# Gate and value of ten pair-stages by seven quarter products, with x, y and the second layer's weights held in DRAM

## The chip, the cores and the metric

The kernel runs on one core of a Trainium2 chip. Five engines work side by side, each through its own queue in order: TensorE (PE in the rows) multiplies matrices into PSUM, VectorE (DVE) and ScalarE (ACT) do elementwise work and are the ones here that read PSUM, GpSimd (POOL) does a little elementwise work on SBUF, and SyncE (SP) issues the DMAs. They wait for each other by semaphores. The time is device microseconds (us) of one execution; the kernel before took 1267.62 us, the median of three runs (1266.94 to 1268.63).

## The reference

One layer of channel attention, and two gated layers one after the other, in float32. N is 6016 tokens, C is 256 channels, d_ff is 1536.

```python
qn = q / (norm(q, axis=tokens) + 1e-6); kn = k / (norm(k, axis=tokens) + 1e-6)
a = softmax(kn.T @ qn / tau, axis=-1)               # 256 x 256
x = v @ a                                           # 6016 x 256
xn = x / sqrt(mean(x * x, axis=-1) + 1e-6) * rms_g  # layer 1
g = xn @ w_gate; y = (silu(g) * (xn @ w_val)) @ w_out
g = y @ w_gate2; out = (sigmoid(g) * (y @ w_val2)) @ w_out2   # layer 2
```

## The kernel before

**Tiles.** The 47 tiles of 128 tokens are cut into twelve blocks: eleven of 512 tokens and one (block 5) of 384. d_ff is cut into twelve slices f of 128. Activations stand transposed, channels on partitions, in two halves c of 128. Every float32 operand of a product is split into a high part, rounded to the multiplier's format by a cast on ACT, and a low part, the rest, subtracted on DVE; a product is three matmuls, high by high, high by low, low by high (`mm3`, lines 86 to 89).

**An item** is one block at one slice of one layer: 288 in all. `emit_gv` makes gate (two products, c = 0 and 1) and value (two) in PSUM banks `g` and `v`, twelve matmuls. `emit_h` takes silu or sigmoid of the gate on ACT (`sg`, L331), multiplies on DVE (L334), casts the hidden value to `hh` on ACT (L337) and subtracts `hl` on DVE (L342). `emit_o`, two items later (`SKEW`), adds the slice's share to the block's output: two products, six matmuls into `y` or `at` (the same `mm3` lines). After slice 11 `emit_evac` copies the two banks out, for layer 1 into `ymid`, which holds all of y in SBUF, for layer 2 into a tile that SP stores. `g` and `v` have two PSUM banks each, `y` and `at` two each: all eight.

**The head** scores k by q while they stream in, makes the softmax matrix (`a_h`, `a_l`, L498 and L499), and then x of blocks 0 and 1. x of a block: `load_v`, split of v (L201, L207), 24 matmuls of 256 columns (L221 to L223), squares with a running sum on ACT (L244), mean on DVE (`ms`, L246), power on POOL (`rs`, L249), scaling (L255, L257), eight transposes (L274), split with rms_g (L282, L284). Blocks 2 to 11 do this between the items of the block before, by `hooks` on item numbers.

**Weights** come as 64-bit floats and are converted on the chip, one slice at a time: three passes on ACT (L119, L123, L136), four on DVE (L129, L139, L144, L147), then the split (L154 on ACT, L159 on DVE). `queue` cuts this into steps, and `pump` emits one to three steps an item. Layer 1's twelve conversions lie in the first 24 items, where blocks 0 and 1 take turns; layer 2's lie in the last two blocks of layer 1. The order of each engine is the order in which the code is written (`manual_schedule`).

## Time and profile before

| | us |
|---|---|
| Median of three runs | 1267.62 |
| The profiled execution, reported time | 1269.37 |
| Its span, first to last instruction | 1267.6 |
| PE busy | 1249.1 (99%) |
| DVE, ACT, POOL busy | 594.8 (47%), 517.1 (41%), 20.7 (2%) |

The reported time of the profiled execution is 1.77 us more than its span, and 1.75 us more than the median. A matmul's recorded time includes its way through the array, so records overlap; the distance from start to start is what a matmul costs in a row of them. The mean clock granted to PE is 0.997 of full.

### The profile page before, as it was taken

The numbers are of one execution on the slowest core, as the hardware profiler recorded it, in microseconds if no ns is written. First come the engines' busy times: TensorE is split into PE (matmuls) and PEld (weight loads), VectorE is DVE, ScalarE is ACT, GpSimd is POOL, SyncE is SP. The second block draws the span as 40 slices with busy tenths as digits, with TensorE's granted clock in tenths as the row PEclk, the third lists the DMA queues.
The fourth block names the chain that finished last, engine by engine and source line by source line (L and its number), as shares of the span: only waits on it lengthen the run. The fifth ranks groups of instructions, "written<-read, shape, count | busy, mean of one in ns | idle before, by whom it ended". The sixth has DMA issues, their size and how long they took to land.

```text
span 1267.6 us, 14204 instructions
## 1 busy us (share of the span) xinstructions
PE 1249.1 (99%) x5758; PEld 1049.7 (83%) x5758; DVE 594.8 (47%) x858; ACT 517.1 (41%) x907; POOL 20.7 (2%) x35
## 2 busy tenths in 40 slices
PE   8889999999999999999999999999999999999998
PEld 7767788888998888888888888888888888888888
DVE  6878643333434434334688534333433333333333
ACT  6766443333333333334567423333333323233332
POOL 0100000000000000000000000000000000000000
PEclk9999999999999999999999999999999999999999
DMA  9523000000000002000222000000000000000000
GB/s 335 213 92 117 18 13 1 18 1 17 17 1 18 17 1 92 1 1 1 67 88 70 1 1 17 17 18 1 17 17 1 17 17 1 17 18 1 17 17 13
DMA packets 15953, 44.42 MB, mean 35 GB/s; under 512 B 1808, under 2 KB 3344, under 8 KB 15888
## 3 DMA queue, kind: packets, MB, share of 16 engines
q1 hardware_dynamic: 15744, 43.39, 9.8%
q8 instruction: 45, 0.74, 0.3%
q14 instruction: 20, 0.16, 0.0%
q10 hardware_dynamic: 144, 0.13, 0.0%
HBM read 37.36 MB, written 6.16 MB: 34 GB/s over the span
## 4 chain that ended last, share of the span: by engine, by line
PE 91%; DVE 3%; ACT 3%; DMA 2%; issue 1%; SPq 0%; POOL 0%; DVEq 0%
PE g L89 10%; PE v L89 10%; PE v L87 10%; PE v L88 10%; PE g L87 10%; PE g L88 10%; PE y L89 9%; PE y L88 9%; PE y L87 9%; DMA in<-in_q_dram 2%; PE y L398 1%; PE at L88 1%; PE at L89 1%; PE at L87 1%; PE at L221 1%
## 5 line engine op out<-in xcount | busy, mean ns | idle before, releaser
L334 DVE TENSOR_TENSOR v<-v,sg 128x512 f32<-128x512 f32 (+1 forms) x288 | 198.0, 687 | 430.8 <-PE v L89 405.2
L337 ACT CAST hh<-v 128x512 fp32r<-128x512 f32 (+1 forms) x288 | 166.4, 578 | 405.7 <-DVE v L334 405.7
L331 ACT ACTIVATE sg<-g 128x512 f32<-128x512 f32 (+1 forms) x288 | 170.0, 590 | 282.5 <-PE g L89 282.4
L342 DVE TENSOR_TENSOR hl<-v,hh 128x512 fp32r<-128x512 f32 (+1 forms) x288 | 195.6, 679 | 149.2 <-ACT hh L337 148.5
L89 PE MATMUL y<-hh,wl 128*128 128x512 f32 (+1 forms) x504 | 193.6, 384 | 0.0
L88 PE MATMUL y<-hl,wh 128*128 128x512 f32 (+1 forms) x504 | 193.5, 384 | 0.0
L87 PE MATMUL y<-hh,wh 128*128 128x512 f32 (+1 forms) x504 | 193.4, 384 | 0.0
L87 PE MATMUL g<-xh,wh 128*128 128x512 f32 (+1 forms) x288 | 112.6, 391 | 5.7 <-ACT wh L154 5.0
L89 PE MATMUL g<-xh,wl 128*128 128x512 f32 (+1 forms) x288 | 111.9, 388 | 1.0 <-DVE wl L159 1.0
L88 PE MATMUL g<-xl,wh 128*128 128x512 f32 (+1 forms) x288 | 111.3, 386 | 0.3 <-DVE xl L284 0.3
L87 PE MATMUL v<-xh,wh 128*128 128x512 f32 (+1 forms) x288 | 111.1, 386 | 0.0
L89 PE MATMUL v<-xh,wl 128*128 128x512 f32 (+1 forms) x288 | 111.0, 385 | 0.0
L88 PE MATMUL v<-xl,wh 128*128 128x512 f32 (+1 forms) x288 | 111.0, 385 | 0.0
L88 PE MATMUL g<-yl,wh 128*128 128x512 f32 (+1 forms) x288 | 110.7, 384 | 0.0
L89 PE MATMUL g<-yh,wl 128*128 128x512 f32 (+1 forms) x288 | 110.7, 384 | 0.0
L87 PE MATMUL g<-yh,wh 128*128 128x512 f32 (+1 forms) x288 | 110.7, 384 | 0.0
L87 PE MATMUL v<-yh,wh 128*128 128x512 f32 (+1 forms) x288 | 110.7, 384 | 0.0
L88 PE MATMUL v<-yl,wh 128*128 128x512 f32 (+1 forms) x288 | 110.7, 384 | 0.0
L89 PE MATMUL v<-yh,wl 128*128 128x512 f32 (+1 forms) x288 | 110.7, 384 | 0.0
L89 PEld LDWEIGHTS y<-hh,wl 128*128 128x128 f32 x504 | 94.6, 188 | 17.8
L88 PEld LDWEIGHTS y<-hl,wh 128*128 128x128 f32 x504 | 94.6, 188 | 17.8
L87 PEld LDWEIGHTS y<-hh,wh 128*128 128x128 f32 x504 | 94.6, 188 | 17.7
(109 smaller groups left out, 1464.2 us busy)
## 6 DMA issues: line engine op xcount, KB each, us to landing
wraw<-in_w_dram SPq DMA_DIRECT2D x24, 768.0 KB, 4.3
vraw<-in_v_t_dram SPq DMA_DIRECT2D x11, 512.0 KB, 3.8
out_t_dram<-y SPq DMA_DIRECT2D x11, 512.0 KB, 2.7
in<-in_k_dram SPq DMA_DIRECT2D x13, 384.0 KB, 6.4
in<-in_q_dram SPq DMA_DIRECT2D x13, 384.0 KB, 6.7
in<-in_k_dram SPq DMA_DIRECT2D x4, 128.0 KB, 3.9
in<-in_k_dram SPq DMA_DIRECT2D x2, 256.0 KB, 6.3
in<-in_q_dram SPq DMA_DIRECT2D x2, 256.0 KB, 6.4
```

What stands on the lines that cost most here:

```text
L87: nc.tensor.matmul(ps, sh, mh, start=start, stop=False)
L88: nc.tensor.matmul(ps, sh, ml, start=False, stop=False)
L89: nc.tensor.matmul(ps, sl, mh, start=False, stop=stop)
L221: nc.tensor.matmul(ps, h[:, c, ts], a_h[:, c], start=c == 0, stop=False)
L331: nc.scalar.activation(out=sg[:, :w], in_=gp[:, :w], func=(AF.Silu, AF.Sigmoid)[l])
L334: nc.vector.tensor_mul(vp[:, :w], vp[:, :w], sg[:, :w])
L337: nc.scalar.copy(hh[:, :w], vp[:, :w])
L342: nc.vector.tensor_sub(hl[:, :w], vp[:, :w], f32(hh[:, :w]))
L398: nc.tensor.matmul(s_ps[c][:, :C], qk[i0][0][:, i, c * P : (c + 1) * P], qk[i0][1][:, i], start=(i0 + i == 0), stop=(i0 + i == NT - 1),)
```

## The change

Two neighbouring blocks make a pair of 1024 tokens (the pair with block 5: 896), cut into two halves e of 512 (448). With the weights of gate and value as a 2 by 2 matrix of 128 by 128 quarters (A11, A12 gate; A21, A22 value) and the pair's input as a 2 by 2 matrix of quarters (B11, B12, B21, B22: channel half by token half), gate and value of both halves were eight quarter products. They become seven, in Winograd's form of Strassen's scheme, with sums of weight quarters (S1 to S4, made once a slice) and of input quarters (T1 to T4, made once a pair). A **period** (function `period`) is one pair at one slice: seven products (21 matmuls) and the four output products of the period before (12 matmuls), 33 where two items had 36. Some of the sums over products are made by adding in PSUM (Z gets three products, B two), the others on DVE and ACT: a period has eight DVE operations and seven ACT operations on a half, where two items had four and four. In layer 1 the pairs 0 and 1 keep the old items (`plain_gv`, `plain_h`); pairs 2 to 5 of layer 1 and all six of layer 2 run in periods: 48 items and 120 periods.

- **x.** All twelve blocks make x at once, before the first item, in a loop over `blocks` (2 to 10, 0, 11, 1); the transposed, scaled block is written to DRAM (`xd`), and only blocks 0 and 1 stay. Later `q_load` and `pair_load` fetch it. All scaling is on DVE.
- **y** of layer 1 goes to DRAM (`yd`) by `evacuate`, four stores a pair, and is fetched by `pair_load` one pair ahead.
- **A pair's operands.** In the pair before: loads in period 0, three subtractions on POOL in period 2 (a fourth after T1's split), and seven splits, one a period, casts in periods 3 to 9 on ACT and subtractions in 4 to 10 on DVE.
- **Conversions.** All 24 run among the 48 items. Each gets four sums of 128 columns on POOL, two casts on ACT (384 and 128 columns) and two subtractions on POOL. The cast to high goes ahead of the next slice's first passes. Layer 2's converted slices go to DRAM (`w2d`) and are loaded back into the slots of layer 1's slices during that layer's last pair; layer 1's S3 goes to `s3d` and later takes the place of A21. Raw weights have two buffers where they had three.

```diff
-    order = [list(range(NB)), [b for b in range(NB) if b != short] + [short]]
...
+    A11, A12, A21, A22, OUT, S1, S2, S4 = 0, 1, 2, 3, 4, 6, 7, 8
+    S3 = A21
...
+        def sums():
+            t = w["t"]
+            w["s3"] = cv2.tile([P, 1, P], F32, tag="s3", name="s3")
+            nc.gpsimd.tensor_add(t[:, S1], t[:, A21], t[:, A22])
+            nc.gpsimd.tensor_sub(w["s3"][:, 0], t[:, A11], t[:, A21])
+            nc.gpsimd.tensor_sub(t[:, S2], t[:, S1], t[:, A11])
+            nc.gpsimd.tensor_sub(t[:, S4], t[:, A12], t[:, S2])
...
+            steps.append([high, size, units, shifted])
+            steps.append([low])
+            steps.append([s_high, whole, signed])
+            steps.append([s_low, rounded])
+            steps.append([guarded, ss[0], store])
+            if i + 2 < len(conversions):
+                steps[-1].append(partial(load_w, *conversions[i + 2]))
...
+    def pair_sums(l, p):
+        sums.clear()
+        pair_sum(l, p, T1, T3, B11)
+        pair_sum(l, p, T2, B22, T1)
+        pair_sum(l, p, T3, B22, T3)
...
+            Z = gv_bank("g")[:, :w]
+            product(Z, it, B11, A11, True)
+        if pv:
+            pl, pp, pf = pv["it"]
+            pw = hw[pp]
+            nc.vector.tensor_add(pv["g1"], pv["g1"], pv["B"])
+            hh0, hl0 = hidden("hh"), hidden("hl")
+            nc.scalar.copy(hh0[:, :pw], pv["v0"])
+            hid[pl, pp, 0, pf] = hh0, hl0
+        if it:
+            e1 = sp.tile([P, 512], F32, tag="e1", name="e1")[:, :w]
+            nc.scalar.copy(e1, Z)
+        if pv:
+            nc.vector.tensor_sub(hl0[:, :pw], pv["v0"], f32(hh0[:, :pw]))
+            nc.scalar.activation(out=pv["g1"], in_=pv["g1"], func=(AF.Silu, AF.Sigmoid)[pl])
+        if it:
+            A = gv_bank("v")[:, :w]
+            product(A, it, B21, A12, True)
+            nc.vector.tensor_add(A, A, e1)
+            B = s["B"] = gv_bank("g")[:, :w]
+            product(B, it, T1, S1, True)
+            sg0 = ip2.tile([P, 512], F32, tag="sg", name="sg")[:, :w]
+            nc.scalar.activation(out=sg0, in_=A, func=(AF.Silu, AF.Sigmoid)[l])
+        if pv:
+            nc.vector.tensor_mul(pv["v1"], pv["v1"], pv["g1"])
+        if it:
+            product(Z, it, T2, S2, False)
+        for fn in slot.get("DVE", ()):
+            fn()
+        if it:
+            s["g1"] = sp2.tile([P, 512], F32, tag="g1", name="g1")[:, :w]
+            nc.scalar.copy(s["g1"], Z)
+        if pv:
+            hh1, hl1 = hidden("hh"), hidden("hl")
+            nc.scalar.copy(hh1[:, :pw], pv["v1"])
+            nc.vector.tensor_sub(hl1[:, :pw], pv["v1"], f32(hh1[:, :pw]))
+            hid[pl, pp, 1, pf] = hh1, hl1
+        for fn in slot.get("ACT", ()):
+            fn()
+        if it:
+            D = s["v0"] = gv_bank("v")[:, :w]
+            product(D, it, T4, A22, True)
+        for o in outs[:1]:
+            o()
+        if it:
+            product(Z, it, T3, S3, False)
+            e3 = sp.tile([P, 512], F32, tag="e3", name="e3")[:, :w]
+            nc.scalar.copy(e3, Z)
+            s["v1"] = sp2.tile([P, 512], F32, tag="v1", name="v1")[:, :w]
+            nc.vector.tensor_add(s["v1"], B, e3)
+            nc.vector.tensor_sub(D, e3, D)
+        for o in outs[1:]:
+            o()
+        if it:
+            product(B, it, B22, S4, False)
+            nc.vector.tensor_mul(D, D, sg0)
...
+        for n, b in enumerate(blocks):
+            x_mm(b, row_banks(n))
+            if n > 1:
+                t_pe(blocks[n - 2])
+                if blocks[n - 2] > 1:
+                    t_out(blocks[n - 2], n % 2)
...
+            if n:
+                x_scale(blocks[n - 1])
+            if n + 2 < NB:
+                v_high(blocks[n + 2])
+                v_low(blocks[n + 2])
+            x_square(b)
+            if n + 3 < NB:
+                load_v(blocks[n + 3])
+            for fn in spare.pop(0) if spare else ():
+                fn()
...
+        stream = [(0, p, f) for p in range(PLAIN, NP) for f in range(NF)]
+        stream += [(1, p, f) for p in (0, 1, 3, 4, 5, 2) for f in range(NF)]
```

On PE, in the middle of layer 2, an item's last value product and an output product stood like this before (`yh`, `yl` are the block's input, high and low):

```order
L87 MATMUL v<-yh,wh 128x512
L88 MATMUL v<-yl,wh 128x512
L89 MATMUL v<-yh,wl 128x512
L87 MATMUL y<-hh,wh 128x512
L88 MATMUL y<-hl,wh 128x512
L89 MATMUL y<-hh,wl 128x512
```

and the middle of a period now (`xh`, `xl` an operand's parts; the products are S2 by T2 into Z, A22 by T4 into D, one output product, S3 by T3 into Z):

```order
L105 MATMUL g<-xh,wh 128x512
L106 MATMUL g<-xl,wh 128x512
L107 MATMUL g<-xh,wl 128x512
L105 MATMUL v<-xh,wh 128x512
L106 MATMUL v<-xl,wh 128x512
L107 MATMUL v<-xh,wl 128x512
L105 MATMUL y<-hh,wh 128x512
L106 MATMUL y<-hl,wh 128x512
L107 MATMUL y<-hh,wl 128x512
L105 MATMUL g<-xh,wh 128x512
L106 MATMUL g<-xl,wh 128x512
L107 MATMUL g<-xh,wl 128x512
```

The second visit to Z in one period stands nine matmuls after the first, with an ACT copy of the bank to be made between them; before, a bank was filled once and read once.

On DVE, before, x work of a block between the items of the block before it (`v` and `hl` are an item's two operations; POOL makes `rs` between `ms` and `xn`):

```order
L334 TENSOR_TENSOR v<-v,sg 128x512
L342 TENSOR_TENSOR hl<-v,hh 128x512
L246 TENSOR_SCALAR ms<-ssq 128x2 x2
L257 TENSOR_SCALAR xn<-at,rs 128x256 x2
L334 TENSOR_TENSOR v<-v,sg 128x512
L342 TENSOR_TENSOR hl<-v,hh 128x512
```

and now two rounds of the loop over blocks, ahead of the first item:

```order
L330 TENSOR_SCALAR xo<-y,g_sb 128x512 x2
L311 TENSOR_SCALAR xn<-at,rs 128x256 x4
L278 TENSOR_TENSOR vl<-vraw,vh 128x1024
L302 TENSOR_SCALAR ms<-ssq 128x4
L190 TENSOR_TENSOR wl<-wst,wh 128x768
L330 TENSOR_SCALAR xo<-y,g_sb 128x512
L311 TENSOR_SCALAR xn<-g,rs 128x256 x2
L311 TENSOR_SCALAR xn<-v,rs 128x256 x2
L278 TENSOR_TENSOR vl<-vraw,vh 128x1024
L302 TENSOR_SCALAR ms<-ssq 128x4
```

The x work has moved out of the stream of items into a stretch of its own, with a conversion's operation (`wl`) between rounds.

On DVE, one period of a pair now (where two items had `v`, `hl`, `v`, `hl`):

```order
L514 TENSOR_TENSOR hl<-v,hh 128x512
L519 TENSOR_TENSOR v<-v,e_6302 128x512
L525 TENSOR_TENSOR v_6274<-v_6274,g_6255 128x512
L363 TENSOR_TENSOR xl<-xl,xh 128x512
L536 TENSOR_TENSOR hl<-v_6274,hh 128x512
L550 TENSOR_TENSOR v_6340<-g,e_6338 128x512
L551 TENSOR_TENSOR v<-e_6338,v 128x512
L556 TENSOR_TENSOR v<-v,sg 128x512
L506 TENSOR_TENSOR g_6322<-g_6322,g 128x512
```

Eight operations of the period itself, and one split of the next pair (L363).

## Rows read from the trace of the kernel before

**Rows 1.** The page, busy time: engine, us (share of the span), instructions.
```profile
PE 1249.1 (99%) x5758; PEld 1049.7 (83%) x5758; DVE 594.8 (47%) x858; ACT 517.1 (41%) x907; POOL 20.7 (2%) x35
```

**Rows 2.** The page, the chain that ended last, share of the span by engine.
```profile
PE 91%; DVE 3%; ACT 3%; DMA 2%; issue 1%; SPq 0%; POOL 0%; DVEq 0%
```

**Rows 3.** Timeline, one item of layer 2: start, us, engine, line, operation [idle before].
```profile
899.90 0.39 PE L89 MATMUL v<-yh,wl 128*128 128x512 f32 x1
900.12 0.39 PE L87 MATMUL y<-hh,wh 128*128 128x512 f32 x1
...
900.38 0.70 DVE L334 TENSOR_TENSOR v<-v,sg 128x512 f32<-128x512 f32 x1 [2.04 <-PE v L89]
...
901.11 0.59 ACT L337 CAST hh<-v 128x512 fp32r<-128x512 f32 x1 [1.49 <-DVE v L334]
...
904.20 0.39 PE L87 MATMUL y<-hh,wh 128*128 128x512 f32 x1
```

**Rows 4.** Timeline, PE, one item of the 384-token block, from gate to gate.
```profile
1255.74 0.33 PE L87 MATMUL g<-yh,wh 128*128 128x384 f32 x1
...
1258.86 0.33 PE L87 MATMUL g<-yh,wh 128*128 128x384 f32 x1
```

**Rows 5.** Windows: us, busy of PE PEld DVE ACT POOL (instructions), clock, DMA, GB/s.
```profile
60.00:65.00 5.00, 4.04 (x17) 2.56 (x16) 3.75 (x8) 4.04 (x12) 1.21 (x2) 1.00 0.17 73
...
80.00:85.00 5.00, 5.00 (x19) 3.96 (x19) 3.37 (x5) 2.03 (x4) 0.00 (x0) 0.81 0.79 265
61.38:137.06 75.68, 68.26 (x287) 53.38 (x287) 61.54 (x87) 51.30 (x84) 1.36 (x2) 0.98 0.26 87
590.00:690.00 100.00, 100.00 (x449) 82.93 (x448) 74.53 (x104) 63.06 (x100) 1.39 (x2) 1.00 0.22 72
```

**Rows 6.** Timeline, from the softmax matrix to the first gate matmul, and one idle.
```profile
53.70 0.28 PE L221 MATMUL x<-a_h,vh 128*128 128x256 f32 x1
...
54.06 0.28 PE L221 MATMUL at<-a_h,vh 128*128 128x256 f32 x1
...
55.32 0.48 DVE L499 SCALAR_TENSOR_TENSOR a_l<-sc,rsum,a_h 128x256 fp32r<-128x256 f32 x1
...
61.38 0.50 PE L87 MATMUL g<-xh,wh 128*128 128x512 f32 x1 [0.67 <-ACT xh L282]
...
77.66 0.50 PE L87 MATMUL g<-xh,wh 128*128 128x512 f32 x1 [3.73 <-ACT wh L154]
```

**Rows 7.** The chain in order of time: a block's eight transposes.
```profile
168.81 0.87 PE at L274 x8
```

**Rows 8.** Groups by line and shape: count, busy us, mean ns, idle before.
```profile
L159 DVE TENSOR_TENSOR wl<-wst,wh 128x768 fp32r<-128x768 f32 x24 | 23.0, 958 | 21.8 <-ACT wh L154 21.6
...
L244 ACT ACTIVATE xn<-at 128x256 f32<-128x256 f32 x43 | 16.1, 382 | 19.3 <-PE at L223 19.3
...
L207 DVE TENSOR_TENSOR vl<-vraw,vh 128x1024 fp32r<-128x1024 f32 x11 | 13.5, 1224 | 6.4 <-ACT vh L201 6.4
...
L201 ACT CAST vh<-vraw 128x1024 fp32r<-128x1024 f32 x11 | 11.5, 1048 | 0.0
...
L257 DVE TENSOR_SCALAR xn<-at,rs 128x256 f32<-128x256 f32 x22 | 10.5, 481 | 4.3 <-POOL rs L249 4.3
```

**Rows 9.** Timeline, POOL beside DVE, two pairs of powers.
```profile
57.30 0.96 DVE L144 CUSTOM_DVE_ANT_0 wbits<-wbits,wunits 128x1536 uint16<-128x1536 uint16 x1
57.42 2.06 POOL L249 TENSOR_TENSOR rs<-ms,nhalf 128x2 f32<-128x2 f32 x2 [12.20 <-DVE ms L246]
...
63.80 1.36 POOL L249 TENSOR_TENSOR rs<-ms,nhalf 128x2 f32<-128x2 f32 x2 [4.31 <-DVE ms L246]
```

**Rows 10.** Groups by line and shape: POOL's widest operation.
```profile
L379 POOL MEMSET acc<- 128x1536 f32 x1 | 1.4, 1382 | 0.0
```

**Rows 11.** The page, DMA issues: count, KB each, median us to landing.
```profile
wraw<-in_w_dram SPq DMA_DIRECT2D x24, 768.0 KB, 4.3
vraw<-in_v_t_dram SPq DMA_DIRECT2D x11, 512.0 KB, 3.8
```

**Rows 12.** Timeline, the last matmul.
```profile
1263.88 0.34 PE L89 MATMUL y<-hh,wl 128*128 128x384 f32 x1
```

More of the change, by code (lines that the diff above doesn't have):

```diff
@@ new lines, with queue, nothing @@
+    conversions = [(l, f) for l in range(2) for f in range(NF)]
+    def queue(first, late):
+        def nothing():
+            pass
+        high, low, s_high, s_low, store = nothing, nothing, *late
+        for i, (l, f) in enumerate(conversions):
+            if i < first:
+                continue
+            (size, units, whole), (shifted, signed, rounded, guarded), hl, ss = conversion(l, f)
+            steps.append([high, size, units, shifted])
[5 more added lines that the diff above has]
+                steps[-1].append(partial(load_w, *conversions[i + 2]))
+            (high, low), (_, s_high, s_low, store) = hl, ss
+        steps.extend(([high], [low, s_high, s_low, store]))
@@ L246, in x_square @@
+    def x_square(b):
+        xn[b] = lent("xn").rearrange("p c t -> p (c t)").rearrange("p (i c) -> p i c", c=C)
+        ssq, ms, rs = xst[b] = [small.tile([P, TB], F32, tag=t, name=t) for t in ("ssq", "ms", "rs")]
+        for i in range(sizes[b]):
+            nc.scalar.activation(
+                out=xn[b][:, i], in_=xps[b][i // 2][:, i % 2], func=AF.Square, accum_out=ssq[:, i : i + 1]
+            )
+        cs = slice(0, sizes[b])
         nc.vector.tensor_scalar(
@@ new lines, in evacuate, with product, period @@
+        nc.sync.dma_start(out=dst, in_=t[:, :w])
+    slots = deque()
+    def product(ps, it, i, a, start):
+        l, p, f = it
+        h, lo = ops[l, p][i]
+        w = hw[p]
+        mm3(ps[:, :w], wh[l, f][:, a], wl[l, f][:, a], h[:, :w], lo[:, :w], start, True, not start)
+    def period(it, pv, outs, last=False):
+        s = {}
+        slot = slots.popleft() if slots else {}
+        outs = [partial(out_mm, *o, c) for o in outs for c in range(KC)]
+        if it:
+            l, p, f = it
+            w = hw[p]
+            s["it"] = it
+            Z = gv_bank("g")[:, :w]
[51 more added lines that the diff above has]
+            o()
+        if it:
+            product(B, it, B22, S4, False)
+            nc.vector.tensor_mul(D, D, sg0)
+        for fn in slot.get("end", ()):
+            fn()
+        return s
@@ L627 @@
+        for e in range(2):
+            for c in range(KC):
+                evacuate(*stream[-1][:2], e, c, c)
 def kernel(**inputs):
```

603 lines of the change are left out of this document (325 added, 278 removed).

## Prediction, made before the changed kernel was run

> **What bounds the kernel now.** I read the busy times first, then the chain of waits, then a timeline of one item, then windows. PE is busy for 1249.1 of 1267.6 us, DVE for 47% and ACT for 41% [rows 1], and PE holds 91% of the chain that ended last [rows 2]. So the end is set by how many matmuls there are and by the distance between them. That distance comes from one item: the same output matmul starts at 900.12 and at 904.20 [rows 3], so eighteen matmuls of 512 columns take 4.08 us, 0.2267 each. An item of 384 columns takes 1258.86 - 1255.74 = 3.12 us, 0.1733 each [rows 4]; half way, 448 columns are an estimated 0.200. In layer 2 PE never waits: DVE stands idle 2.04 us for PE's value in every item [rows 3]. What PE loses it loses at the start: from the first gate matmul at 61.38 to 137.06 it is busy for 68.26 of 75.68 us at a clock of 0.98 [rows 5], which is 7.4 us idle and 1.5 us of slow clock, because items wait for converted weights.
>
> **Term 1, the periods.** 96 periods are of 512 columns, 24 of 448. At PE's distance they take 96 x 33 x 0.2267 + 24 x 33 x 0.200 = 718.2 + 158.4 = 876.6 us. The same work in items took 96 x 8.16 + 24 x (4.08 + 3.12) = 956.2 us. The gain is 79.6 us, if PE does not wait inside a period.
>
> **Whether it waits.** I lay out one period by hand, t = 0 at its first matmul. A product is three matmuls, 0.68. From the timeline: a reader starts 0.25 after a product's slot ends (the last value matmul starts at 899.90, the next at 900.12, DVE at 900.38); a DVE operation takes 0.70 and an ACT operation 0.59; a handover costs 0.03 (DVE ends 901.08, ACT starts 901.11) [rows 3]. Independent operations of one engine overlap by 0.1. All forms in a period (PSUM with SBUF into either, a cast, an activation) stand in the trace at these durations.
> PE's slots: Z 0 to 0.68, A to 1.36, B to 2.04, Z again to 2.72, D to 3.40, output to 4.08, Z a third time to 4.76, three outputs to 6.80, B again to 7.48.
> - The copy e1 of Z runs 0.93 to 1.52; Z is written again at 2.04. Slack 0.52.
> - B of the period before ends at 0; g1 + B runs 0.25 to 0.95; B's bank is written at 1.36. Slack 0.41.
> - A + e1 starts at 1.61, ends 2.31; sg0 on ACT to 2.93; the copy g1 waits for Z (2.72 + 0.25), ends 3.56; Z is written at 4.08. Slack 0.52.
> - The copy e3 starts at 5.01, ends 5.60; v1 = B + e3 ends 6.33; B is written at 6.80. Slack 0.47.
> - hl0 ends 1.55 (needed at 3.40); hl1, after v1 x g1 (2.91) and hh1 (4.06), ends 4.78 (needed at 5.4).
> DVE's and ACT's own loop (v1, D, D x sg0, g1 + B, hl0, A + e1; sg0, g1, hh1, a split's cast, e3) is 3.9 + 2.7 + 0.1 = 6.7 us of 7.48. With an evacuation or a split in a period it still closes. So I take no wait in term 1. The other bound is that each slack is overrun by 0.1 to 0.35 us a period, 12 to 42 us in all; I take zero since every duration is a row of this trace. What hides the rest: the next pair's loads land (3.8 us for 512 KB [rows 11]) two periods before POOL wants them; the second layer's weights, two loads of 576 KB a period, are wanted eleven periods, 82 us, after they are asked for, against 4.3 us for 768 KB [rows 11]. SP issues in order and waits there for PE of the period just past; stores and loads behind it are late by a period at most, and none is wanted so soon.
>
> **Term 2, x ahead of everything.** `x_mm` now takes both channel halves tile by tile, so it starts in earnest when the second `a_l` is made, 55.32 + 0.48 = 55.8 [rows 6]; I take 55.3, since the first three matmuls go ahead. A block costs PE 24 x 0.12 (three matmuls from 53.70 to 54.06 [rows 6]) + 0.87 for transposes [rows 7] = 3.75 us. It costs DVE one or two `xo` of 0.70 [rows 3], four scalings of 0.39 in a row (0.48 each less the overlap), the split 1.14 (1.22 less it) [rows 8] and the mean, together 3.5 to 4.1; ACT, the cast 1.05 and four squares (0.38 each, with the accumulator's read in its gap) [rows 8], 2.6. A third loop goes over memory: `load_v` stands behind the store of `xo` on SP, lands 3.8 us later [rows 11], and the cast, squares, mean, power, scaling and transposes that follow on it are two rounds on: about 12.0 to 13.5 us for three rounds. The three limits are 3.75, 3.9 and 4.0 to 4.5; I take 4.3. The first two rounds fill until 55.3 + 3 x 2.88 + 0.87 + 0.2 = 65.0; nine rounds of 4.3 end at 103.7; four conversion operations of 0.95 on DVE [rows 8] between rounds add 3.8; block 0's split, block 1's scaling and block 11's transposes add 4.5. **First gate at 112.0**, where it was 61.38. Bounds: 103 (3.75 a round, conversions hidden) and 122 (loads at 6.5 us, 5.0 a round). In before ten blocks of this lay between items and cost PE 37 us there; so the move itself costs 13 us.
>
> **Term 3, the 48 items.** 48 x 4.08 = 195.8, and block 1's transposes 0.9. Conversions: the first gate needs slice f at item 1.6 f, that is every 6.5 us; before, PE lost 8.9 us there [rows 5]. Now the cast comes ahead of two ACT passes, which gives its low part earlier, and two more casts (about 0.7 us by ACT's rows) come into ACT; x no longer disturbs. I take 11 (bounds 0 and 30, see the first rival). Layer 2's twelve conversions lie in 24 items of 4.08, 8.2 us each, with DVE at 4.0 + 2 x 1.3 = 6.6; a denser run of them before left PE at 100.00 of 100 [rows 5]; I take 2. The first pair's operands are loaded five items ahead: 1.
>
> **Term 4, the end.** The last matmul ended at 1264.22 [rows 12], 3.4 us before the span did; that stays. The last period's outputs must wait for silu or sigmoid of the second half: g1 + B, activation, product, cast, subtraction, by the durations above 4.7 us with 2.4 us of matmuls in it: 2.3 us more. Together 5.7.
>
> **Sum.** 112.0 + 195.8 + 0.9 + 11 + 2 + 1 + 876.6 + 5.7 = 1205.0 us of span. The profiled execution's time is 1.77 above its span and 1.75 above the median, so span and median are the same number here: **1205 us**, 62.6 us or 4.9% less.
>
> **The rivals.**
> *POOL and DVE hold each other.* Every conversion now has six POOL operations on 1,024 columns beside DVE operations with two inputs in SBUF. The trace shows one side: a pair of powers took 2.06 us when its first began beside a DVE operation of two SBUF inputs, 57.30 to 58.26, and 1.36 elsewhere [rows 9]; the first waited 0.7 us. The trace has no row in which DVE waited, and none of POOL's additions. Bounds for six of them: 0.9 us at the memset's 0.9 ns a column [rows 10], 5.9 us at 0.68 an operation [rows 9] plus two memsets' rate. DVE is nearly full only in the first ten conversions; half of the middle, 1.7 us each, gives 17 us: 1222. The Trainium skill, page "SBUF — State Buffer", section "Who interferes with whom", says that a VectorE instruction with two SBUF inputs and a GpSimd instruction that reads SBUF exclude each other, and that the one that comes second waits to the end of the first; by that rule DVE would wait as POOL did, and the trace agrees for POOL's side.
> *The slack in a period is eaten.* Some wait of 0.1 to 0.35 us in each of 120 periods, at e1, g1, e3 or B: 1217 to 1247. For it: four places with half a microsecond. Against it: the layout above.
> *x at half clock.* After 3.73 us idle the clock fell (0.81 in 80 to 85) [rows 5, 6]. At 1.2 GHz a round is 7.5 us of PE, 9 x 3.2 = 29 us more: 1234. Against it: PE with idle pieces kept 1.00 from 60 to 65 [rows 5], and no idle in the loop is over 2 us.
> *Slower than before.* Seven ACT and eight DVE operations a period hang in one loop of eleven; PE pays for nothing while the loop is under 7.48 us. At 7.48 + 62.6/120 = 8.0 us the gain is gone. That needs 0.12 us more on each of the eleven than the rows show, as when PSUM is read twice as often beside PE's writes: at 8.1, 1279. Nothing in the trace shows such a stretch.
> *It does not do what it says:* the matmuls fall, but PE is bound elsewhere and the time stays within 0.2%. I find no such bound; it needs 0.5 us in each period exactly.
>
> **How the numbers follow.** My forecast, 1192 to 1218, has 0.62; POOL 0.14; slack 0.09; half clock 0.05; slower 0.07; the same 0.03. A difference under 0.2% cannot be told from none here. Faster by over 0.2%: 0.62 + 0.14 + 0.09 + 0.05 = 0.90. The range goes from 1190 (x at its lower bound, conversions at 6) to 1240, which takes in POOL, half clock and most of the slack case.
>
> **What would show it.** Right: matmul distances of 0.227 through a whole period, 7.48 us from one Z to the next; first gate near 112; PE idle in the x stretch about 15%. Wrong: PE waiting for `e1`, `g1`, `e3` or `v1` in the waits (term 1); rounds above 5 us, or PE waiting there for a v load (term 2); DVE operations at twice their length beside POOL (term 3). If periods take over 8 us, all of it is wrong.

## The result and the profile after

The changed kernel took 1215.45 us (median of four runs, 1215.33 to 1217.14) where the kernel before took 1268.12 beside it: a ratio of 0.9585, 95% interval 0.9566 to 0.9603. The gain is 52.7 us of the 62.6 that were forecast. The profiled execution, the longest of the four, reports 1217.14 us, with a span of 1215.3.

On the page, the busy times and the chain that ended last (they answer to [rows 1, 2]):

```profile
PE 1183.3 (97%) x5398; PEld 989.9 (81%) x5398; DVE 936.6 (77%) x1397; ACT 733.0 (60%) x1348; POOL 178.2 (15%) x207
...
PE 71%; DVE 1%; ACT 1%; DMA 0%; issue 0%; ACTq 0%; DVEq 0%
```

TensorE has 360 matmuls less, 65.8 us less of busy time, and still holds the chain (which could be followed back through 73% of the span). DVE, ACT and POOL have taken over the additions: 342, 216 and 158 us more.

One period of 512 columns in the middle of layer 2, from the timeline (start, duration, engine, line, operation, output and inputs; idle time before it in brackets). It answers to the item of [rows 3]:

```profile
735.79 0.39 PE L105 MATMUL g<-xh,wh 128*128 128x512 f32 x1
735.99 0.69 DVE L506 TENSOR_TENSOR g<-g,g 128x512 f32<-128x512 f32 x1
...
736.73 0.59 ACT L512 COPY e<-g 128x512 f32<-128x512 f32 x1
...
737.15 0.39 PE L105 MATMUL g<-xh,wh 128*128 128x512 f32 x1
...
737.83 0.39 PE L105 MATMUL g<-xh,wh 128*128 128x512 f32 x1
...
738.77 0.59 ACT L532 COPY g<-g 128x512 f32<-128x512 f32 x1
...
739.87 0.39 PE L105 MATMUL g<-xh,wh 128*128 128x512 f32 x1
...
740.81 0.59 ACT L548 COPY e<-g 128x512 f32<-128x512 f32 x1 [0.42 <-PE g L107]
...
741.43 0.69 DVE L550 TENSOR_TENSOR v<-g,e 128x512 f32<-128x512 f32 x1 [0.83 <-ACT e L548]
...
742.59 0.39 PE L105 MATMUL g<-xh,wh 128*128 128x512 f32 x1
...
743.27 0.39 PE L105 MATMUL g<-xh,wh 128*128 128x512 f32 x1
```

From the first Z at 735.79 to the next at 743.27 it is 7.48 us, 33 times 0.2267, and no matmul in it waits. The four places of the layout by hand can be read off (e1, g1 and e3 are ACT's copies of Z, v1 is the second half's value). The copy e1 ends at 737.32 and Z is written again at 737.83: 0.51 to spare (0.52 forecast). g1 + B ends at 736.68 and B is written at 737.15: 0.47 (0.41). The copy g1 ends at 739.36, Z is written at 739.87: 0.51 (0.52). v1 ends at 742.12, B is written at 742.59: 0.47 (0.47).

The stretch of the 48 items, from the first gate matmul (110.71) to the first Z (323.87), in windows (engine busy times and instruction counts, granted clock, DMA share, GB/s), and TensorE's waits in it (the wait for `hl` is for the bank `v`, which is free when `hl` has been read from it):

```profile
110.71:323.87 213.16, 202.81 (x863) 162.36 (x862) 173.46 (x225) 142.53 (x246) 109.77 (x141) 0.98 0.50 175
110.71:130.00 19.29, 16.32 (x65) 12.71 (x64) 14.67 (x21) 12.16 (x21) 8.62 (x11) 0.86 0.26 84
130.00:240.00 110.00, 102.62 (x430) 80.25 (x429) 96.90 (x119) 78.19 (x133) 63.28 (x82) 0.98 0.48 167
240.00:323.87 83.87, 83.87 (x372) 69.40 (x371) 61.89 (x86) 52.17 (x93) 37.88 (x48) 1.00 0.59 206
```

```profile
PE g L105 <- ACT wh L182: 5.2, 3, 2.1
PE v L105 <- DVE hl L451: 2.6, 4, 1.8
PE g L107 <- DVE wl L190: 2.5, 4, 0.9
```

All that is lost is lost before 240: TensorE is idle for 10.4 us there, and the granted clock is 0.86 and 0.98. How the idle time and the clock hang together is in one place of the timeline:

```profile
124.33 0.50 PE L105 MATMUL g<-qh,wh 128*128 128x512 f32 x1 [2.07 <-ACT wh L182]
...
125.97 0.61 PE L107 MATMUL g<-qh,wl 128*128 128x512 f32 x1 [0.90 <-DVE wl L190]
126.38 0.63 PE L105 MATMUL g<-qh,wh 128*128 128x512 f32 x1
126.80 0.63 PE L106 MATMUL g<-ql,wh 128*128 128x512 f32 x1
```

TensorE waits 2.07 us for the third slice's cast and 0.90 for its low part, and then its matmuls come 0.42 apart instead of 0.23, the lower of its two levels (1.2 GHz), until 129.4: after 3.0 us of waiting, eight matmuls that cost some 1.6 us more than in a period. Part of a wait there is paid a second time. In the kernel before the same stage lost 7.4 us idle at a clock of 0.98 [rows 5].

**The account** of the profiled span, with the forecast's terms cut at the same places (the last two items' twelve output matmuls lie in the first period, so the forecast's first Z is at 320.0, and the last period's outputs come after the last product):

| | forecast | measured | difference |
|---|---|---|---|
| First gate matmul | 112.0 | 110.71 | -1.3 |
| From there to the first Z | 208.0 | 213.16 | +5.2 |
| First Z to the end of the last product | 876.6 | 882.05 | +5.4 |
| From there to the end of the span | 8.4 | 9.4 | +1.0 |
| Span | 1205.0 | 1215.3 | +10.3 |

How much of this is chance can be read from the other profiled runs below. In the six with the same head and x stage (this one, e3_no_t4, e4_short, e7_e3x3, e8_whole_first, e11_late_high) the first gate matmul comes between 110.0 and 113.0. In the five with the same items (this one, e3_no_t4, e4_short, e5_loads, e7_e3x3) the stretch to the first Z is 212.3 to 213.9.

### The profile page after: what moved, and what is told of

The parts are those of the page before. It is cut to its first block, busy times and chain, and to the rows that moved or that the text cites. A ratio compares the mean times of both kernels' runs of the same rounds, so it can differ in the third digit from the quotient of the medians.

```text
span 1215.3 us, 15199 instructions
## 1 busy us (share of the span) xinstructions
PE 1183.3 (97%) x5398; PEld 989.9 (81%) x5398; DVE 936.6 (77%) x1397; ACT 733.0 (60%) x1348; POOL 178.2 (15%) x207
## 4 chain that ended last, share of the span: by engine, by line
PE 71%; DVE 1%; ACT 1%; DMA 0%; issue 0%; ACTq 0%; DVEq 0%
PE g L105 11%; PE g L106 11%; PE g L107 11%; PE at L106 4%; PE at L107 4%; PE at L105 4%; PE v L106 4%; PE v L107 4%; PE y L106 4%; PE v L105 4%; PE y L107 4%; PE y L105 4%; DMA out_t_dram<-yo 0%; DVE hl L536 0%; DVE v L556 0%
## 5 line engine op out<-in xcount | busy, mean ns | idle before, releaser
L508 ACT CAST hh<-v 128x512 fp32r<-128x512 f32 (+1 forms) x120 | 69.2, 577 | 237.9 <-DVE v L556 237.9
L536 DVE TENSOR_TENSOR hl<-v,hh 128x512 fp32r<-128x512 f32 (+1 forms) x120 | 89.1, 742 | 96.4 <-ACT hh L535 96.4
L105 PE MATMUL g<-qh,wh 128*128 128x512 f32 (+1 forms) x276 | 108.2, 392 | 5.2 <-ACT wh L182 5.2
L106 PE MATMUL at<-hl,wh 128*128 128x512 f32 (+1 forms) x288 | 111.9, 389 | 0.3 <-DVE hl L536 0.2
L105 PE MATMUL y<-hh,wh 128*128 128x512 f32 (+1 forms) x288 | 111.0, 386 | 0.7 <-ACT hh L508 0.7
L106 PE MATMUL y<-hl,wh 128*128 128x512 f32 (+1 forms) x288 | 111.0, 386 | 0.2 <-DVE hl L514 0.2
L105 PE MATMUL at<-hh,wh 128*128 128x512 f32 (+1 forms) x288 | 111.1, 386 | 0.0
L107 PE MATMUL at<-hh,wl 128*128 128x512 f32 (+1 forms) x288 | 111.0, 385 | 0.0
L107 PE MATMUL g<-qh,wl 128*128 128x512 f32 (+1 forms) x276 | 108.1, 392 | 2.5 <-DVE wl L190 2.5
L106 PE MATMUL g<-ql,wh 128*128 128x512 f32 (+1 forms) x276 | 107.3, 389 | 0.0
L105 PE MATMUL v<-qh,wh 128*128 128x512 f32 (+1 forms) x216 | 85.2, 394 | 2.6 <-DVE hl L451 2.6
L556 DVE TENSOR_TENSOR v<-v,sg 128x512 f32<-128x512 f32 (+1 forms) x120 | 82.3, 686 | 4.2
```

The source lines that it names most:

```text
L105: nc.tensor.matmul(ps, sh, mh, start=start, stop=False, skip_group_check=more)
L106: nc.tensor.matmul(ps, sh, ml, start=False, stop=False, skip_group_check=more)
L107: nc.tensor.matmul(ps, sl, mh, start=False, stop=stop, skip_group_check=more)
L508: nc.scalar.copy(hh0[:, :pw], pv["v0"])
L536: nc.vector.tensor_sub(hl1[:, :pw], pv["v1"], f32(hh1[:, :pw]))
L556: nc.vector.tensor_mul(D, D, sg0)
```

## Experiments

All times are medians, except where one run is named; ratios are to the kernel before, run on the same chip. The changed kernel's 1215.45 has 0.9566 to 0.9603, which is what each is to be held against.

### The items: GpSimd, then ACT

For its size, the term that was furthest off is that of the items. Two kernels take away what the sums of weights cost there, first GpSimd's part, then ACT's too.

In the first the six GpSimd operations go, and the casts read plain quarters (the low parts of the sums are then not stored and fetched either):

```diff
-            nc.gpsimd.tensor_add(t[:, S1], t[:, A21], t[:, A22])
...
-            nc.gpsimd.tensor_sub(t[:, S4], t[:, A12], t[:, S2])
...
-            nc.scalar.copy(h[:, S1:], w["t"][:, S1:])
+            nc.scalar.copy(h[:, S1:], w["t"][:, :3])
...
-            nc.gpsimd.tensor_sub(lo[:, S1:], w["t"][:, S1:], f32(h[:, S1:]))
...
-            nc.gpsimd.tensor_sub(w["3l"], w["s3"], f32(w["3h"]))
```

> Leaves out what GpSimd does in a weight conversion (four sums and two low parts, six operations of 128 to 384 columns); the casts on ACT stay and read the plain quarters instead, and the products take plain quarters, so the output is not the reference's. Theory 1 (VectorE waits for GpSimd): the shift, the sign operation and the low part fall from 726, 1115 and 1096 ns to the 552, 951 and 958 of the kernel before, 0.5 us a conversion; in the ten that feed the items this is on the path: the stretch from the first gate matmul to the first product falls from 213.3 to about 207, 1208 to 1211 us in all. Theory 2 (the loss is the length of the conversion chain itself, GpSimd only fills VectorE's gaps): within 1.5 us of 1215.4.

Measured: 1211.81 us, 0.9551 to 0.9577, which overlaps the changed kernel's interval, so the median alone doesn't show a gain. In the profiled runs the first gate matmul moves little (110.95), and from there to the first Z it is 207.5 us where it was 213.16, and 212.3 at least with the same items. The groups of VectorE's operations from 110 to 320, first of the changed kernel, then of this one (count, busy time, mean ns):

```profile
L451 DVE TENSOR_TENSOR hl<-v,hh 128x512 fp32r<-128x512 f32 x46 | 31.4, 684 | 9.4 <-ACT hh L445 9.3
L156 DVE SCALAR_TENSOR_TENSOR wbits<-wraw,wbits 128x768 uint32<-128x768 uint32 x22 | 24.9, 1130 | 0.0
L161 DVE CUSTOM_DVE_ANT_0 wbits<-wbits,wunits 128x1536 uint16<-128x1536 uint16 x22 | 21.7, 987 | 8.0 <-ACT wunits L153 7.3
L146 DVE TENSOR_SCALAR wbits<-wraw 128x768 uint32<-128x768 uint32 x22 | 16.3, 742 | 0.0
...
L190 DVE TENSOR_TENSOR wl<-wst,wh 128x768 fp32r<-128x768 f32 x10 | 11.3, 1125 | 0.1
```

```profile
L441 DVE TENSOR_TENSOR hl<-v,hh 128x512 fp32r<-128x512 f32 x48 | 33.0, 687 | 12.3 <-ACT hh L435 12.3
...
L156 DVE SCALAR_TENSOR_TENSOR wbits<-wraw,wbits 128x768 uint32<-128x768 uint32 x22 | 20.9, 949 | 0.0
L146 DVE TENSOR_SCALAR wbits<-wraw 128x768 uint32<-128x768 uint32 x22 | 12.1, 551 | 0.0
...
L185 DVE TENSOR_TENSOR wl<-wst,wh 128x768 fp32r<-128x768 f32 x10 | 9.5, 951 | 0.1
```

Without GpSimd the sign operation falls from 1130 to 949 ns, the shift from 742 to 551, the low part from 1125 to 951 (958 in [rows 8]): 0.55 us a conversion. The subtraction `hl`, which has one input in PSUM, stays at 684 to 687. So VectorE does wait for GpSimd, at operations with two inputs in SBUF and at the shift, and hardly elsewhere (the rounding falls from 987 to 957, the guard from 961 to 951). It costs 5.65 us of the items: TensorE is idle 2.8 us less, and its matmuls take 2.9 us less (202.81 and 199.93). VectorE and ACT hardly wait for a result of GpSimd in the changed kernel's conversions (ACT's cast 0.7 us in all), so its operations are held while GpSimd's run, and don't wait for a result. Theory 1 holds, near to its number.

The Trainium skill, page "SBUF — State Buffer", section "Who interferes with whom", says that a VectorE instruction with at most one SBUF input does not contend with GpSimd unless it runs in a two-port mode, which copies, casts and tensor_scalar can enter; the 684 against 687 of `hl` and the 742 against 551 of the shift, a tensor_scalar, agree with both halves.

In the second, beside that, the casts go, and what stores and fetches the sums:

```diff
-            nc.scalar.copy(h[:, S1:], w["t"][:, :3])
...
-            nc.scalar.copy(w["3h"], w["t"][:, 3:4])
...
-                nc.sync.dma_start(out=s3d[f][:, 0], in_=f32(w["3h"])[:, 0])
-                nc.sync.dma_start(out=s3d[f][:, 1], in_=f32(w["3l"])[:, 0])
```

> As e1_no_pool, and the two casts of the sums on ACT (0.51 and 0.30 us a conversion) and their stores are left out too; the products take plain quarters, so the output is not the reference's. Theory 1 (ACT's casts stand ahead of the items' silu and cast): 2 to 4 us less than e1_no_pool. Theory 2 (ACT has room, 73% busy in this stretch): within 1 us of e1_no_pool. In the prediction this was the 2 us or so by which the conversions were to cost more than before, less the cast that comes earlier.

Measured: 1205.10 us, 0.9497 to 0.9523, 6.7 less than e1_no_pool and more than either theory gave; from the first gate matmul to the first Z it is 200.95. Two casts that ACT makes in 0.81 us a conversion, with their stores, cost 6.6 us. What goes with them is a wait of VectorE's rounding (L161) for ACT's pass back to whole numbers (`wunits`, L153). Its rows in e1_no_pool and in e2_no_sums:

```profile
L161 DVE CUSTOM_DVE_ANT_0 wbits<-wbits,wunits 128x1536 uint16<-128x1536 uint16 x22 | 21.1, 957 | 9.2 <-ACT wunits L153 8.7
```

```profile
L161 DVE CUSTOM_DVE_ANT_0 wbits<-wbits,wunits 128x1536 uint16<-128x1536 uint16 x22 | 21.0, 957 | 1.8 <-ACT wunits L153 1.2
```

The casts stood ahead of that pass in ACT's queue, and 8.7 us of VectorE's waiting became 1.2. Theory 1 had the cost at the items' own silu and cast, and VectorE's waits for those stayed as they were (10.5 and 11.5 us for `sg`, 11.6 and 11.1 for `hh`). That the wait for the pass is the path is tested next.

### The casts put behind the pass

One line of `queue`:

```diff
-            steps.append([s_high, whole, signed])
+            steps.append([whole, s_high, signed])
```

> In the conversion queue the cast of the sums (ACT, 0.51 and 0.30 us) goes behind the pass that takes the units back to whole numbers (ACT, 0.85 us), on which VectorE's rounding waits; nothing is left out. Theory 1 (the 6.7 us that the two casts cost go by VectorE's wait for that pass, 8.0 us in all in the kernel after the change, 1.8 without the casts): that wait falls to 3 us or less and the time by 3 to 6 us, 1209 to 1212. Theory 2 (the casts stand in the way of the items' own silu and cast, or of the weights' high part, wherever they are put): within 1.5 us of 1215.4.

Measured: 1212.16 us, 0.9543 to 0.9586: 3.3 less by the medians, with intervals that overlap. In the profiled run the items' stretch is 209.95 us, 2.4 below the shortest with the same items and 3.2 below the changed kernel's. VectorE's groups in this kernel:

```profile
L161 DVE CUSTOM_DVE_ANT_0 wbits<-wbits,wunits 128x1536 uint16<-128x1536 uint16 x22 | 25.1, 1140 | 0.9
L164 DVE SCALAR_TENSOR_TENSOR wst<-wst,wbits 128x768 f32<-128x768 f32 x22 | 24.2, 1098 | 0.5
L156 DVE SCALAR_TENSOR_TENSOR wbits<-wraw,wbits 128x768 uint32<-128x768 uint32 x22 | 21.6, 984 | 0.0
```

The wait for `wunits` is gone, as theory 1 has it. But the rounding now takes 1140 ns instead of 987 and the guard (L164) 1098 instead of the 961 it had, while the sign operation falls from 1130 to 984: GpSimd's two subtractions follow the casts, so they moved on with them, from beside one VectorE operation to beside two others. Of 8.0 us of waits 0.9 is left, 6.5 came back in those two operations, and 3.3 went from the sign operation. Most of what the order gained in waits it lost again in longer operations.

### The cast of the high part

Another line of `queue`:

```diff
-            steps.append([high, size, units, shifted])
+            steps.append([size, units, high, shifted])
```

> The cast of a slice's high part goes back behind the two ACT passes of the next slice (0.9 us each), where it was in the kernel before; nothing else changes and nothing is left out. Theory 1, the prediction's (with the cast ahead the low part comes earlier, which pays for the two casts of the sums): TensorE's waits for the high and the low part grow from 5.2 and 2.5 us by 1 to 1.8 in each conversion that is waited for, 4 to 10 us more in all, 1219 to 1226. Theory 2 (it only trades with the next slice's passes): within 1.5 us of 1215.4.

Measured: 1217.41 us, 0.9582 to 0.9623, 2.0 more by the medians, and the intervals overlap. In the profiled run, its slowest, it is 215.3 from the first gate matmul to the first Z, 1.4 above the longest with the same items. TensorE waits 7.4 us for the high part instead of 5.2, but 0.8 instead of 2.5 for the low part. So the sign is likely the prediction's and the reason is not: the earlier cast helps the high part, and the low part, which the prediction had it help, is waited for longer. Its worth, some 2 us by these runs and hardly outside their scatter, is half of the smallest that was expected, against the 6.6 of the sums' casts.

### The loads of v

In the x loop, with one more load ahead of it (`load_v(blocks[3])` after the second block's `v_low`):

```diff
-            if n + 3 < NB:
-                load_v(blocks[n + 3])
+            if n + 4 < NB:
+                load_v(blocks[n + 4])
```

> Each load of a block of v is issued one round of the x stage earlier (the buffer is free by then); nothing else changes. Theory 1 (the loop over memory is the longest of the three limits of a round): ACT's 13.9 us of waits for these loads go, rounds fall from about 4.3 to 3.9 us, the first gate matmul comes at 106 to 107 instead of 110.7, and the end at 1210 to 1213. Theory 2 (VectorE with its conversions is as long as the load loop): the waits move to VectorE, the first gate comes at 109.5 to 111 and the time stays within 1.5 us of 1215.4.

ACT's longest waits in the x stage, of the changed kernel and of this one:

```profile
ACT vh L272 <- DMA vraw<-in_v_t_dram: 13.9, 7, 3.1
```

```profile
ACT vh L272 <- DMA vraw<-in_v_t_dram: 2.1, 3, 0.7
```

The first gate matmul comes at 105.14 instead of 110.71. Not all of that need be the edit's: the first x matmul was already at 50.28 instead of 52.07 (49.3 to 54.3 in the profiled runs). From there to the first gate it is 54.9 us instead of 58.6, 3.8 less. The transposes of one block follow those of the block before after 4.42 us instead of 4.82, in the mean of eight rounds (64.84 to 100.23, and 66.64 to 105.16). So the loop over memory was the longest of the three limits, as term 2 has it. The median is 1214.24 (0.9565 to 0.9593): by that it can't be told from the changed kernel. Its profiled run was its fastest (1211.66, clock 0.998), with 213.0 us from first gate to first Z; where the others, at clocks of 0.993 to 0.997, lost more, the one trace doesn't show.

### The hand-over from x to the items

What stood ahead of the first item goes behind items 0 and 1:

```diff
-        x_scale(1)
-        t_pe(NB - 1)
-        t_out(NB - 1, 1)
...
+        def t_side():
+            t_pe(NB - 1, at_bank)
+            t_out(NB - 1, 1)
+
+        hook(0, x_scale, 1)
         hook(0, t_last)
+        hook(1, t_side)
```

> Block 11's transposes and the scaling of block 1 go behind the first item's gate and value, so the first gate matmul follows block 0's split at once. Theory 1 (TensorE's idle 2.3 us and the transposes' 1.0 us, with the slow clock behind them, are lost for good): first gate at 107 to 108, 1210 to 1212 us. Theory 2 (the third slice's cast, on which the fourth item waits at 124.3, is set by VectorE's and ACT's own queue, not by TensorE): the first gate is earlier, but the wait for slice 2's cast grows by as much, 1214 to 1216 us.

Measured: 1222.08 us, 0.962 to 0.9656, 6.6 slower, which neither theory had. The first gate matmul did come earlier, at 106.63. Then, in the timeline:

```profile
111.98 0.89 ACT L136 ACTIVATE wst<-wraw 128x768 f32<-128x768 f32 x1 [2.51 <-POOL wl L204]
...
113.55 0.58 ACT L445 CAST hh<-v 128x512 fp32r<-128x512 f32 x1
114.16 0.69 DVE L451 TENSOR_TENSOR hl<-v,hh 128x512 fp32r<-128x512 f32 x1 [3.14 <-ACT hh L445]
114.77 1.65 DVE L311 TENSOR_SCALAR xn<-at,rs 128x256 f32<-128x256 f32 x4
115.38 2.41 PE L318 MATMUL y<-ident,xn 128*128 128x128 f32 x8 [5.16 <-DVE xn L311]
```

This is read from below. TensorE waits 5.16 us for block 1's scaling; the scaling stands behind the first item's `hl` on VectorE; `hl` waits 3.14 for the cast `hh`; `hh` stands on ACT behind a conversion's first pass, which waits 2.51 for the buffer that GpSimd is still reading. I had moved a step that could have started at 111.0, when GpSimd had made its `rs`, behind one that hung on three other queues. The granted clock from 110 to 120 is 0.83, and the items' stretch, with these transposes in it, 222.0 us.

### The slack in a period, from both sides

The first lengthens the loop at one of the four places:

```diff
-            nc.scalar.copy(e3, Z)
+            for _ in range(3):
+                nc.scalar.copy(e3, Z)
```

> The copy e3 of the third Z is made three times instead of once, so v1 comes 1.0 to 1.2 us later in each period; nothing is left out. Theory 1 (the slack there is 0.47 us, as the prediction has it): each period grows by 0.5 to 0.7 us, 1276 to 1300 us, and TensorE waits for v1 ahead of the last product into B. Theory 2 (the slack is over 1.2 us): periods stay at 7.48. Theory 3 (there is no slack): 1.0 to 1.2 more, 1335 to 1360 us.

TensorE's longest wait (us in total, times, longest), and one place of the timeline:

```profile
PE g L105 <- DVE v L551: 75.7, 120, 0.9
```

```profile
703.96 0.39 PE L107 MATMUL at<-hh,wl 128*128 128x512 f32 x1
...
704.26 0.69 DVE L551 TENSOR_TENSOR v<-g,e 128x512 f32<-128x512 f32 x1 [2.10 <-ACT e L549]
...
705.01 0.50 PE L105 MATMUL g<-zh,wh 128*128 128x512 f32 x1 [0.66 <-DVE v L551]
705.34 0.39 PE L106 MATMUL g<-zl,wh 128*128 128x512 f32 x1
```

Measured: 1332.52 us in one run, with periods of 8.43 us, 0.95 longer. By its time alone this run lies next to theory 3 (no slack, 1335 us), but the wait and its length are theory 1's, in each of 120 periods. The size was off because three copies in a row take 1.83 us (I had let them overlap), 1.24 more than one: 1.24 - 0.47 is 0.77, TensorE's next matmul starts 0.82 late (705.01 instead of 704.19), and the matmul behind it comes 0.33 later instead of 0.23, another 0.1.

The second shortens TensorE's part; in the periods' `out_mm` one matmul of three is kept for each output:

```diff
-        mm3(
-            yacc[l, p, e][c][:, :w], wh[l, f][:, OUT + c], wl[l, f][:, OUT + c],
-            hh[:, :w], hl[:, :w], f == 0, f == NF - 1,
-        )
+        nc.tensor.matmul(ps, wh[l, f][:, OUT + c], (hl if c else hh)[:, :w], start=f == 0, stop=f == NF - 1)
```

> Leaves out eight of the twelve output matmuls of each of the 120 periods (one of three is kept for each output), so a period has 25 matmuls and the output is not the reference's; VectorE, ACT and GpSimd do all that they did. Theory 1 (the loop over VectorE and ACT takes 6.7 us, as the prediction's layout has it, and hides behind 33 matmuls): periods of 512 columns take 6.6 to 6.8 us, 1120 to 1132 us in all, TensorE waits for v1 or e3 in each. Theory 2 (the loop is much shorter than laid out): 25 times 0.2267, 5.7 us a period, near 1010 us. Theory 3 (the loop is the bound already, and 7.48 is only by chance 33 times 0.2267): 7.4 us, over 1200.

Its longest wait of TensorE in the periods, and places of one period, from one last product into B to the next (the copy g1, the third product into Z and the copy e3 between them):

```profile
PE g L105 <- DVE v L558: 71.2, 109, 0.9
```

```profile
702.00 0.50 PE L105 MATMUL g<-xh,wh 128*128 128x512 f32 x1 [0.68 <-DVE v L558]
...
705.79 0.59 ACT L540 COPY g<-g 128x512 f32<-128x512 f32 x1
...
706.44 0.48 PE L105 MATMUL g<-xh,wh 128*128 128x512 f32 x1
...
707.48 0.59 ACT L556 COPY e<-g 128x512 f32<-128x512 f32 x1
...
708.85 0.50 PE L105 MATMUL g<-xh,wh 128*128 128x512 f32 x1 [0.67 <-DVE v L558]
```

Measured: 1146.53 us in one run. With 25 matmuls a period takes 6.85 us and TensorE waits for v1. So the loop is 6.85 us, not the 6.7 of the layout, and it hides behind 7.48 with 0.63 to spare. It isn't the layout's loop, though, which has only VectorE and ACT in it and a split's cast among ACT's operations: the periods without a split take 6.85 us too. The third product into Z starts when the copy g1 has ended (706.38), and e3 starts after that product, so TensorE has a part in the loop, 1.1 us from the end of g1 to the start of e3, and the cast fits beside it. The pairs of 448 columns take 6.2 us; with them the time comes out above the 1132 that I gave. The rival in which the loop reaches 8.0 us is out by more than a microsecond; at the same time this kernel is nearly at its floor: fewer output matmuls would bring at most 0.63 us a period.

The third takes away GpSimd's one sum beside a period's split, in `pair_low`:

```diff
-            pair_sum(l, p, T4, T2, B21)
+            sums[T4] = sums[T2]
```

> Leaves out GpSimd's fourth sum of a pair of blocks (1.29 us, once in twelve periods; the third sum's values stand in, so the output is not the reference's). Theory 1 (VectorE's hl1, both inputs in SBUF, waits for it: 1.53 us instead of 0.69, and TensorE for hl1): the wait of TensorE for hl1, 2.9 us in ten, goes, and the ten periods fall from about 7.6 to 7.48, 1 to 3 us in all. Theory 2 (the wait is from the split that stands there on VectorE): it stays.

In the changed kernel's timeline:

```profile
355.58 1.29 POOL L392 TENSOR_TENSOR xs<-xs,ql 128x512 f32<-128x512 f32 x1 [14.43 <-DVE ql L363]
355.82 1.53 DVE L536 TENSOR_TENSOR hl<-v,hh 128x448 fp32r<-128x448 f32 x1 [0.47 <-ACT hh L535]
```

From one copy e3 to the next it is 7.48 us, and in eight periods, once a pair, 7.58 to 7.86 (7.04 instead of 6.69 in one of 448 columns). Without that sum eight of these nine fall to the usual length, the ninth from 7.86 to 7.76; together 1.3 us. The one run took 1216.10, span 1214.3. Theory 1 is right, and small. It is the same hold as in the conversions: v1 and hh1 both lie in SBUF, and the one place in a period where that meets GpSimd pays.

### Together

The edits of e5_loads and e8_whole_first, and the hand-over with block 1's scaling left in its place:

```diff
         x_scale(1)
-        t_pe(NB - 1)
-        t_out(NB - 1, 1)
...
         hook(0, t_last)
+        hook(1, t_side)
```

> Three edits together, nothing left out: loads of v one round earlier (as e5_loads), the cast of the sums behind the pass to whole numbers (as e8_whole_first), and block 11's transposes and scaling after the second item, in the banks of at, with block 1's scaling left where it was (e6_handoff had it moved behind the first item on VectorE, and TensorE waited 5.2 us for it). Theory 1 (the gains add: 5.6 us earlier at the first gate, 3 us in the conversions, 2 to 3 us at the hand-over): 1204 to 1208 us. Theory 2 (VectorE sets both stretches, so what TensorE gains at the hand-over it waits for at the third and fourth slice): 1209 to 1212, as e8_whole_first or e5_loads alone.

Measured: 1208.22 us (1207.81 to 1211.02), 0.9517 to 0.955, which lies wholly below the changed kernel's interval: 7.2 us less by the medians and 6.6 by the ratios, just past the upper edge of theory 1. The first gate matmul comes at 100.91, 9.8 us earlier; from the first x matmul to it, it is 51.4 us instead of 58.6, so 7.3 us are the edits' and the rest is the head. The stretch from there to the first Z, now with block 11's transposes in it, is as long as it was:

```profile
100.91:314.36 213.45, 203.33 (x869) 162.85 (x870) 181.55 (x232) 145.05 (x255) 114.33 (x141) 0.98 0.51 174
```

So the 3.2 us that e8_whole_first gained there are gone again, with the transposes and a wait for block 1's scaling in the stretch. VectorE is busy for 181.55 us in it; without GpSimd's sums (e1_no_pool) it is busy for 162.7 in its 207.5.

Two more kernels, on top of e9_all, tried to shorten that stretch. One moves a conversion out of it; `late[0]` holds the third slice's steps, and `more` runs the first three:

```diff
+        spare += [
+            [*ss0[2:], partial(more, 0)],
+            [lambda: late[0][0][2](), lambda: late[0][1][1]()],
+            [ss1[1], lambda: late[0][1][2]()],
+            [*ss1[2:], lambda: late[0][1][3](), lambda: late[0][3][0](), partial(load_w, 0, 4)],
+            [lambda: late[0][2][0]()],
+        ]
...
-        queue(2, ss1[1:])
+        queue(3, late[0][3][1:])
```

> As e9_all, and the conversion of the third slice goes into the last five rounds of the x stage, where VectorE is busy for 46 of 55 us. Theory 1 (the items' first waits, for the third slice, are the start of the whole queue of conversions and one slice more ahead of them takes 4 to 5 us of VectorE's work out of the stretch in which it is the bound): 3 to 6 us less than e9_all. Theory 2 (the x stage becomes longer by what VectorE gets to do there): within 1.5 us of e9_all.

Measured: 1208.18 us, 0.9511 to 0.9554. The items' stretch is 4.1 us shorter (209.3), and from the first x matmul to the first gate it is 5.3 us longer (56.7): theory 2.

The other changes the order of the first two blocks' items:

```diff
-        ahead = 3 * [0, 0, 1, 0, 1] + [0, 0, 1, 0]
+        ahead = [0, 0, 1, 1] + 3 * [0, 0, 1] + [0, 1, 0, 0, 1, 0]
```

> As e9_all, and the first two blocks' items in another order: block 1's first two slices come before block 0's third, so the third slice is wanted at the fifth item instead of the fourth, the fifth slice at the eighth instead of the seventh, the others where they were; nothing is left out. Theory 1 (what TensorE waits for there are single slices that come an item too late: 1.9 us for the third slice's cast in e9_all): 2 to 4 us less than e9_all, 1204 to 1206. Theory 2 (VectorE works at its limit from the first item on, so a wait that is taken away here returns at a later slice): within 1.5 us of 1208.2.

Measured: 1207.19 us, 0.9509 to 0.955. TensorE's waits for the high part are 3.4 us as they were 3.3, but in three places instead of two, and those for `hl` 3.1 in six instead of 2.6 in four: theory 2, in that a wait that is taken away at one slice returns at another. That VectorE is at its limit is not shown by this: it is busy for 182.2 of the 212.8 us and waits for ACT in most of the rest, so it looks as if the two bind in turn.

## Why the prediction was right, and where it was off

**Term 1 was right.** TensorE waits for nothing in a period, but for hl1 once a pair; the four slacks are those laid out from rows of the kernel before, to 0.06 us. That they are slack e7_e3x3 shows for v1, and e4_short for a period as a whole. In the loop that hides behind the matmuls the layout left out TensorE's third product into Z (e4_short). The 5.4 us that it was short are 2.1 for the pairs of 448 columns (their period is 6.69, so 0.2027 a matmul; half way between 512 and 384 I had estimated 0.200), 1.3 for GpSimd's fourth sum, 0.5 at the change of layer, where ACT loads another table for 1.28 us, and 1.2 at the first Z, where TensorE waits for the split of its second operand. I had written that all forms in a period stand in the trace; v1 x g1 and hl1 have both inputs in SBUF, which none of those rows has.

**Term 2 was right**, and for the reason given: e5_loads shows the loop over memory to be the limit of a round. Eight of its rounds took 4.82 us each in the mean, conversions with them, where nine of 4.3 and 3.8 for conversions make 4.72; TensorE was idle for 12% of the stage where I gave 15%. That it came out to 1.3 us is in part luck, since the first gate varies by 3 us between runs of the same stage.

**Term 3 was the step that failed in size.** I took 14 us for what the conversions lose and the trace gives 19.1 (213.16 less 852 x 0.2267 and the transposes' 0.9). 10.4 of that are idle time and 8.7 matmuls further apart. By the experiments 5.65 is VectorE waiting for GpSimd, 6.55 the two casts of the sums, and 6.9 what is lost without either. I had set the casts at 0.7 us of ACT's time, let the earlier cast of the high part pay for them, and not asked which VectorE operation waits behind them in ACT's queue. The earlier cast pays some 2, and not by the low part (e11_late_high).

**The first rival was a true mechanism with too high a price.** VectorE does wait for GpSimd, for 0.55 us a conversion and not 1.7. GpSimd's six operations are long enough, 4.7 us together (518, 500, 825, 687, about 1050 and 1100 ns by the trace's groups), near the upper of my bounds; but VectorE waits for little of that. Of their 107.6 us in the stretch 31 lie beside the items' two operations with an input in PSUM, which aren't held, and 13 beside no work of VectorE. In the 61 beside a conversion's operations it is often GpSimd that waits: the subtraction of 128 columns (L209) takes 1.07 to 1.13 us, most of it beside the rounding, which goes only from 957 to 987 ns, and 0.46 without VectorE beside it (111.91 in e6_handoff). It cost 5.65 us where I gave 17. The time alone, 10 us above the forecast and 7 below this rival's 1222, couldn't tell the two apart; the rows do.

**Slack eaten, x at half clock, slower:** none of them. The clock in the x stage was 0.99 as a whole. What did fall is the clock in the items (0.86 up to 130), after idle pieces of 2.27 us before the first gate and of 2.07 and 0.90 later; the prediction had such a fall only for the x stage.

**Term 4** was short by 1.0 us. The fourth copy of the last outputs waits for a buffer:

```profile
1211.89 0.53 ACT L473 COPY yo<-at 128x448 f32<-128x448 f32 x1 [2.63 <-DMA out_t_dram<-yo]
```

`yo` has three buffers, and the last period stores four tiles; the last matmul ended at 1210.65.

## What to carry to other kernels

When work is taken from the busiest engine and given to the others, lay out one period by hand from durations of the trace, with each buffer's last reader and next writer: here it gave the period of 512 columns to 0.01 us and each slack to 0.06. Follow the loop behind the matmuls through TensorE's own products too. Where the other engines are nearly full, price an added operation not by its own length but by what stands behind it in its queue and who waits for that: two casts, 0.81 us a conversion, cost 6.6 us in all, largely by the pass that stood behind them, and a scaling moved behind one item made TensorE wait 5.2 us. And before putting sums on GpSimd, look at which VectorE operations beside them have both inputs in SBUF, or were lengthened here with one, as the shift; the new order tried here moved that hold and didn't remove it.

## What the runs showed of the chip that was not expected

- VectorE's shift with one input in SBUF (L146) takes 551 ns without GpSimd beside it and 742 with it. I had looked only at operations with two.
- A wait of TensorE costs about 0.1 us more than its length: the matmul behind the first one follows after 0.33 us instead of 0.23 (705.01 to 705.34 in e7_e3x3, 702.00 to 702.34 in e4_short).
- Idle pieces of 2.07 and 0.90 us close together were followed by 3 us of matmuls at the lower level of the clock, 0.42 us apart.
- A matmul of 448 columns comes every 0.2027 us where one of 512 comes every 0.2267 and one of 384 every 0.1733 [rows 3, 4].
- Loads take longer in the changed kernel: `vraw` 4.7 us from issue to landing where it was 3.8, `wraw` 4.9 where it was 4.3 [rows 11]. No run separates why.
